# Soft-capped attention with a SoLU feed-forward block on one core: values in 32-column tiles, reciprocals of the row sums through HBM, a tabled order of steps

## The chip, the cores and the metric

The kernel runs on one core of a Trainium2 chip. Times are device microseconds (us) of one execution. The kernel before takes 423.69 us, the median of 3 runs (423.61 to 424.09). "Engines" are PE (TensorE matmul), PEld (its weight loads), DVE (VectorE), ACT (ScalarE), POOL (GpSimd) and SP (the queue that issues nearly all DMAs).

## What is computed

```
scores = (q @ k.T) / sqrt(64);  scores = cap * tanh(scores / cap)
attn   = exp(scores - max) / (sum(exp(scores - max)) + 1e-9)
x      = attn @ v                         # 4 batches, 12 heads, 448 tokens, 64 per head
h      = x @ w_in                         # 1792 x 768 times 768 x 1024
solu   = h * softmax(h)
ln     = (solu - mean) / sqrt(var + 1e-6) * g_ln
out    = ln @ w_out                       # 1792 x 1024 times 1024 x 768
```

All inputs and the output are float32.

## The kernel before, in words

The 48 heads are worked on in pairs: 24 units (6 per batch). For a unit PE makes the transposed scores of both heads in three chunks of 128 keys and one rest of 64 (`scores`, L391, `scores_rest`, L396); the scores are split into three float32r products (hi·hi, hi·lo, lo·hi), so a chunk is six matmuls in two row tiles. ACT applies tanh (L401, L419) and exp (L404). `values` (L472) multiplies the exponentials by v, one step per chunk of keys, each head in one column tile of 64; `values_rest` (L477) adds the rest. These are plain float32 matmuls, each recorded as two MATMUL records. `rowsums` (L486) multiplies the same exponentials by a selector of 32 columns, so that the row sums of head j of pair hp land in row hp of a 32-row region of one PSUM tile `z`. From unit 8 on (`ADDS_FROM`) DVE first adds the three chunks and the rest (L451, L457, L455), which leaves 4 instead of 16 row-sum matmuls for a pair of units.

`divide` ends a batch: ACT adds a guard (L535), one float32 matmul with the constant `both` (L536) adds the two regions of each head and repeats them, DVE takes reciprocals in four column parts (L541), and for each part and each of the six pairs a `stream_shuffle` (L544) spreads one row over the partitions and a multiply (L545) scales the attention output `xt`.

The feed-forward block works on 14 tiles of 128 tokens: `ff_in` splits the tile in two float32r terms (L567, L568), 36 matmuls (L577 to L579), SoLU and layer norm on DVE, ACT and POOL (L584 to L624), a transpose by DVE (L627) and four DMAs (L632, `ef<-h`); `ff_out` is 48 matmuls (L666 to L668), a copy (L675) and a store (L678). In the first batches DVE and ACT also prepare the weights (L712 to L722).

The order of all this is made when the program is built. Every piece is a step of `Plan` with an engine, a cost, a due time and the steps it needs; `Plan.run` is a list scheduler that emits the steps in the order of its own estimated starts, and each engine then works through its instructions in that order and waits where data are not ready. A step on PE also has a tile shape (`tiling`): 64x128 for scores, 128x64 for values, 128x32 for row sums, 64x64 for the rests, 128x128 for the rest of the program.

## Time and profile before

| | |
|---|---|
| median of 3 runs | 423.69 us |
| the profiled execution's own time | 423.13 us |
| its span, first to last instruction | 421.2 us |
| PE busy | 405.1 us (96%) |
| DVE busy | 298.3 us (71%) |
| ACT busy | 243.6 us (58%) |
| POOL busy | 57.6 us (14%) |

The rows further down come from the profiled execution, and sums are made against its 423.13 us. A row of a timeline gives a start, a duration and, in brackets, idle time before it and what ended that. Matmuls overlap: the distance between two starts is the price of the first, the duration is not. Busy time of PE is the union of overlapping records.

### The profile page before, as it was taken

The page shows a single profiled execution, that of the slowest core. Times are in us where ns is not written, and L with a number is a line of the kernel's source. Part 1 is how long each engine was busy: PE and PEld are TensorE (multiplying, and loading weights), DVE is VectorE, ACT ScalarE, POOL GpSimd, SP SyncE. Part 2 cuts the span into 40 slices and gives each one's busy share as a digit, 9 for nine tenths or more (in the row PEclk, how much of TensorE's full clock was granted, in tenths as well). Part 3 has the DMA queues.
Part 4 walks back from the last instruction along what each step waited for, and adds up shares of the span by engine and source line. Part 5 has one row for each costly group of instructions (what it writes and reads, how often), then busy time and mean ns, then how long its engine had stood idle before and what let it go on. Part 6 is the DMA issues. An engine that isn't in the chain of part 4 may idle for free.

```text
span 421.2 us, 6343 instructions
## 1 busy us (share of the span) xinstructions
PE 405.1 (96%) x2292; PEld 279.7 (66%) x2292; DVE 298.3 (71%) x725; ACT 243.6 (58%) x322; POOL 57.6 (14%) x122
## 2 busy tenths in 40 slices
PE   8689999999989999999999999999999999999993
PEld 4234345657734368696875696586677898998993
DVE  2999889998997899955556399964463996544510
ACT  4799998678878984625377556764911222212210
POOL 2000000144220001211130020130211101211200
PEclk9899999999999999999999999999999999999997
DMA  7878872021424230403224024031030202122031
GB/s 268 355 264 283 309 257 97 2 53 64 121 65 150 70 129 19 135 1 86 69 86 134 3 86 133 23 111 43 2 87 0 80 28 68 44 65 70 20 110 44
DMA packets 24265, 42.46 MB, mean 101 GB/s; under 512 B 3744, under 2 KB 17568, under 8 KB 24224
## 3 DMA queue, kind: packets, MB, share of 16 engines
q1 hardware_dynamic: 24080, 41.76, 31.3%
q8 instruction: 20, 0.33, 0.3%
q10 hardware_dynamic: 144, 0.20, 0.1%
q14 instruction: 21, 0.17, 0.1%
HBM read 29.10 MB, written 5.51 MB: 82 GB/s over the span
## 4 chain that ended last, share of the span: by engine, by line
PE 80%; DVE 9%; ACT 5%; POOL 2%; issue 2%; ACTq 0%; POOLq 0%; DVEq 0%
PE pv L472 11%; PE s L391 9%; PE m L666 9%; PE m L668 9%; PE m L667 9%; PE m L577 8%; PE m L579 8%; PE m L578 8%; PE s L396 4%; PE z L486 4%; DVE o L714 1%; DVE o L715 1%; PE pv L753 1%; ACT eb L404 1%; POOL st L617 1%
## 5 line engine op out<-in xcount | busy, mean ns | idle before, releaser
L666 PE MATMUL m<-wo,ln 128*128 128x384 f32 x208 | 71.2, 342 | 0.0
L668 PE MATMUL m<-wo,ln 128*128 128x384 f32 x208 | 69.9, 336 | 0.0
L667 PE MATMUL m<-wo,ln 128*128 128x384 f32 x208 | 69.7, 335 | 0.0
L577 PE MATMUL m<-wi,xh 128*128 128x512 f32 x168 | 66.4, 395 | 0.0
L579 PE MATMUL m<-wi,xl 128*128 128x512 f32 x168 | 65.8, 392 | 0.0
L578 PE MATMUL m<-wi,xh 128*128 128x512 f32 x168 | 65.7, 391 | 0.0
L600 POOL TENSOR_SCALAR st<-st 128x1 f32<-128x1 f32 x14 | 14.1, 1010 | 285.1 <-ACT ef L595 285.1
L401 ACT ACTIVATE ea<-s 128x896 f32<-128x896 f32 x48 | 41.7, 926 | 9.5 <-PE s L391 9.5
L472 PE MATMUL pv<-ea,v 128*64 128x448 f32 x192 | 42.8, 565 | 3.8 <-ACT ea L404 3.3
L675 ACT COPY o<-m 128x384 f32<-128x384 f32 x26 | 12.5, 480 | 56.3 <-PE m L668 56.3
L404 ACT ACTIVATE ea<-ea 128x1792 f32<-128x1792 f32 x24 | 41.0, 1710 | 0.3
L666 PEld LDWEIGHTS m<-wo,ln 128*128 128x128 f32 x208 | 39.0, 188 | 3.1 <-issue 1.6
L667 PEld LDWEIGHTS m<-wo,ln 128*128 128x128 f32 x208 | 39.1, 188 | 1.0 <-issue 0.4
L668 PEld LDWEIGHTS m<-wo,ln 128*128 128x128 f32 x208 | 39.0, 188 | 0.3 <-DVE ln L656 0.3
L595 ACT ACTIVATE ef<-h,st 128x1024 f32<-128x1024 f32 x14 | 16.1, 1153 | 39.6 <-DVE h L584 31.6
L577 PEld LDWEIGHTS m<-wi,xh 128*128 128x128 f32 x168 | 31.5, 188 | 9.5 <-issue 2.2
L579 PEld LDWEIGHTS m<-wi,xl 128*128 128x128 f32 x168 | 31.5, 188 | 7.0 <-DVE xl L568 0.4
L578 PEld LDWEIGHTS m<-wi,xh 128*128 128x128 f32 x168 | 31.5, 188 | 6.0
L391 PEld LDWEIGHTS s<-hi 64*128 64x128 f32 x138 | 12.9, 183 | 30.2 <-issue 13.1
L404 ACT ACTIVATE eb<-eb 128x1344 f32<-128x1344 f32 x24 | 32.2, 1341 | 0.4
L391 PE MATMUL s<-hi 64*128 64x448 f32 x138 | 30.2, 434 | 1.0 <-ACT eb L419 1.0
L472 PEld LDWEIGHTS pv<-ea,v 128*64 128x64 f32 x192 | 11.9, 138 | 26.3 <-issue 16.6
(114 smaller groups left out, 745.4 us busy)
## 6 DMA issues: line engine op xcount, KB each, us to landing
raw<-in_kq SPq DMA_DIRECT2D x24, 448.0 KB, 3.5
ef<-h SPq DMA_DIRECT2D x56, 128.0 KB, 2.7
wo<-in_w_out SPq DMA_DIRECT2D x15, 384.0 KB, 6.4
wi<-in_w_in SPq DMA_DIRECT2D x11, 512.0 KB, 7.5
v<-in_v SPq DMA_DIRECT2D x24, 224.0 KB, 2.6
out<-o SPq DMA_DIRECT2D x27, 192.0 KB, 1.9
ln<-in_w_in SPq DMA_DIRECT2D x1, 512.0 KB, 6.9
es<-in_w_out SPq DMA_DIRECT2D x1, 384.0 KB, 5.0
```

Of the source, the lines that this page charges most:

```text
L391: nc.tensor.matmul(pt.get()[:, j, :S], lhsT=x[half[j], c * P:(c + 1) * P], rhs=y[half[j], NC * P:], start=(i == 0), stop=(i == len(parts) ...
L396: nc.tensor.matmul(pt.get()[p.place[j], 0, :S], lhsT=x[half[j], :REST], rhs=x[half[j], S:], start=True, stop=True)
L401: step("ACT", act(2 * S, 0.11), at, lambda: nc.scalar.activation(out=p.chunk(c), in_=pt.get()[:, :, :S], func=AF.Tanh, scale=r_tanh), [pt] ...
L404: step("ACT", act(k * S), at, lambda: nc.scalar.activation(out=e.get(), in_=e.get(), func=AF.Exp, scale=r_exp), [e], [e])
L472: nc.tensor.matmul(t[half[j], :S], lhsT=vv[:, j * NC + c], rhs=p.chunk(c)[:, j], start=(c == 0), stop=False, skip_group_check=True)
L486: nc.tensor.matmul(zt[b].get()[r:r + 32, :S], lhsT=w, rhs=buf.get()[:, c], start=r not in zbegun[b], stop=not left[r], skip_group_check=Tr ...
L577: nc.tensor.matmul(pt.get(), lhsT=a, rhs=w[:, 0], start=(kk == 0), stop=False)
L578: nc.tensor.matmul(pt.get(), lhsT=a, rhs=w[:, 1], start=False, stop=False)
L579: nc.tensor.matmul(pt.get(), lhsT=l, rhs=w[:, 0], start=False, stop=(kk == KD - 1))
L666: nc.tensor.matmul(p, lhsT=a, rhs=w[:, 0], start=(f == 0), stop=False)
L667: nc.tensor.matmul(p, lhsT=a, rhs=w[:, 1], start=False, stop=False)
L668: nc.tensor.matmul(p, lhsT=l, rhs=w[:, 0], start=False, stop=(f == KF - 1))
```

## The change

Three things change in the work and one in its order.

- `values` makes four matmuls per chunk, each with 32 columns of v, in place of two with 64; its tile shape is then 128x32, that of the row sums.
- `divide` takes the reciprocal of all 448 columns at once into SBUF, stores them in an HBM tile `zd`, and loads them back for each part, broadcast over 64 partitions (`rs`, now one buffer for six pairs); one multiply scales a part of all six pairs. In batches whose row sums are added on DVE first (`one`: here batches 1 to 3) the `both` matmul is gone, since each head then has one region. A part is two load DMAs in batch 0 and four in batches 1 to 3.
- `ADDS_FROM` goes from 8 to 6: units 6 and 7 are added on DVE too. Only one buffer is left for `xh`.
- The order is no longer computed: `tabled` emits the steps in the order of a table, which also names the engine of each copy.

```diff
-ADDS_FROM = 8
+ADDS_FROM = 6
+XHN = 1
+RSN = 1
+ORDER = """
+01000H0W0d02WI050J03120X070Y06040Z0e0S0A0a08190fWb130g0K0B140p0c09150M0h1Z160C0DWiX70E0j1A240L180G1B0NWq1g1C0F1a1D0O0P2i
...
+    def tabled(self):
+        code = [LETTERS.index(x) for x in "".join(ORDER.split())]
+        order = [64 * x + y for x, y in zip(code[::2], code[1::2])]
+        for i in order:
+            n = self.steps[i % 2048]
+            if n["eng"] == self.COPY:
+                n["emit"](self.copy["DVE" if i >= 2048 else "ACT"])
+            else:
+                n["emit"]()
...
-    rz_r, rs_r = ring("rz", 1, [P, most]), ring("rs", 2, [P, most])
-    xh_r, xl_r = ring("xh", 2, [P, KD, P], F32R), ring("xl", XLS, [P, KD, P], F32R)
+    rs_r = ring("rs", RSN, [P, NP, most])
+    xh_r, xl_r = ring("xh", XHN, [P, KD, P], F32R), ring("xl", XLS, [P, KD, P], F32R)
...
             for j in range(2):
-                nc.tensor.matmul(t[half[j], :S], lhsT=vv[:, j * NC + c], rhs=p.chunk(c)[:, j], start=(c == 0), stop=False, skip_group_check=True)
+                for r in (0, 32):
+                    nc.tensor.matmul(t[j * D + r:j * D + r + 32, :S], lhsT=vv[:, j * NC + c, r:r + 32], rhs=p.chunk(c)[:, j], start=(c == 0), stop=False, skip_group_check=True, tile_position=(0, j * D + r))
...
-        zs, z = es_r.new(), z_r.new()
+        zs, one = es_r.new(), not general and b * NP >= ADDS_FROM
...
+        if not one:
+            z = z_r.new()
+            step("PE", MM448_F32, due, lambda: nc.tensor.matmul(z.get()[:, :S], lhsT=both, rhs=zs.get()[:, 0], start=True, stop=True), [zs], [z])
+        zd = Buf(lambda: dram.tile([P, S], F32, name=f"zd{b}"))
+        step("DVE", 0.0064 * S, due, lambda: nc.vector.reciprocal(out=zs.get()[:, 1], in_=zs.get()[:, 0] if one else z.get()[:, :S]), [zs] if one else [zs, z], [zs])
+        step("SP", 0.5, due, lambda: nc.sync.dma_start(out=zd.get(), in_=zs.get()[:, 1]), [zs], [zd], lag=2.2)
...
-                step("DVE", dve(n), due + part * LATER, lambda rs=rs, rz=rz, hp=hp, n=n: nc.vector.stream_shuffle(out=rs.get()[:, :n], in_=rz.get()[:, :n], mask=[hp] * 32), [rz], [rs])
-                step("DVE", dve(n), due + part * LATER, lambda rs=rs, hp=hp, sl=sl, n=n: nc.vector.tensor_mul(xt[b].get()[:, hp, sl], xt[b].get()[:, hp, sl], rs.get()[:, :n]), [rs, xp], [xp])
+            def spread(rs=rs, sl=sl, n=n):
+                for j in range(2):
+                    r = zd.get()[j * D:(j + 1) * D]
+                    if one:
+                        for g in range(2):
+                            nc.sync.dma_start(out=rs.get()[half[j], g::2, :n], in_=r[g * 33:g * 33 + NP - 1:2, sl].partition_broadcast(D))
+                    else:
+                        nc.sync.dma_start(out=rs.get()[half[j], :, :n], in_=r[:NP, sl].partition_broadcast(D))
+
+            step("SP", 1.7 if one else 0.9, due + part * LATER, spread, [zd], [rs], lag=2.5)
+            step("DVE", dve(NP * n), due + part * LATER, lambda rs=rs, sl=sl, n=n: nc.vector.tensor_mul(xt[b].get()[:, :, sl], xt[b].get()[:, :, sl], rs.get()[:, :, :n]), [rs, *xps], xps)
...
-        plan.run()
+        plan.run() if general else plan.tabled()
```

The table moves instructions on every engine. Three places matter below. In the rows "x2" means two such instructions in succession; line numbers of the kernel before and of the changed one differ.

The start of PE's program, before (`pv` is the output of values, `z` of row sums, `s` of scores):

```order
L753 MATMUL pv<-xtail 128x256 x5
L396 MATMUL s<-raw 64x448 x2
L386 MATMUL s<-raw 128x448 x6
L472 MATMUL pv<-ea,v 64x448 x4
L472 MATMUL pv<-eb,v 64x448 x2
L486 MATMUL z<-ea,sel 32x448 x4
L486 MATMUL z<-eb,sel 32x448 x2
L486 MATMUL z<-eb,sel_64 32x448
L486 MATMUL z<-eb,sel_65 32x448
L391 MATMUL s<-hi 128x448 x2
L391 MATMUL s<-lo,hi 128x448 x2
L391 MATMUL s<-hi,lo 128x448 x2
```

and now:

```order
L793 MATMUL pv<-xtail 128x256 x5
L429 MATMUL s<-raw 64x448 x2
L419 MATMUL s<-raw 128x448 x6
L424 MATMUL s<-hi 128x448 x2
L424 MATMUL s<-lo,hi 128x448 x2
L424 MATMUL s<-hi,lo 128x448 x2
L424 MATMUL s<-hi 128x448 x2
L424 MATMUL s<-lo,hi 128x448 x2
L424 MATMUL s<-hi,lo 128x448 x2
L506 MATMUL pv<-ea,v 32x448 x8
L520 MATMUL z<-ea,sel 32x448 x4
L520 MATMUL z<-eb,sel 32x448 x2
```

Two score chunks of unit 1 have moved ahead of the values of unit 0.

DVE between the reciprocals of batch 0 and the first multiply that uses them, now (the reciprocal, L574, stands four rows above the first of these; L759 to L768 prepare weights, L408 casts the scores' input):

```order
L408 CAST hi<-raw 128x832
L760 SCALAR_TENSOR_TENSOR o<-wo_501,o 128x384
L768 SCALAR_TENSOR_TENSOR wo_748<-o,gT,wo_748 128x384
L759 TENSOR_SCALAR o<-o 128x384
L761 SCALAR_TENSOR_TENSOR o<-wo_501,o 128x384
L760 SCALAR_TENSOR_TENSOR o<-wo_512,o 128x384
L759 TENSOR_SCALAR o<-o 128x384
L761 SCALAR_TENSOR_TENSOR o<-wo_512,o 128x384
L760 SCALAR_TENSOR_TENSOR o<-wo_620,o 128x384
L768 SCALAR_TENSOR_TENSOR wo_814<-o,gT,wo_814 128x384
L768 SCALAR_TENSOR_TENSOR wo_817<-o,gT,wo_817 128x384
L591 TENSOR_TENSOR xt<-xt,rs 128x6x128
```

Before, reciprocal, shuffles and multiplies of a part followed one another; now 14 other instructions stand between the reciprocal and the first multiply.

SP around the same place, now (`zd` is the store of the reciprocals, `rs` their loads; `v` and `raw` are loads of later units):

```order
L455 DMA v<-in_v 128x448
L401 DMA raw<-in_kq 128x896
L575 DMA zd_758<-es 128x448
L588 DMA rs<-zd_758 64x6x128 x2
L455 DMA v<-in_v 128x448
L401 DMA raw<-in_kq 128x896
L588 DMA rs<-zd_758 64x6x128 x4
L588 DMA rs<-zd_758 64x6x64 x2
L455 DMA v<-in_v 128x448
L401 DMA raw<-in_kq 128x896
```

The store and the loads of all four parts now stand between loads of `v` and `raw` for later units.

## Rows read from the trace of the kernel before

**Rows 1.** Stretches: length; PE, PEld, DVE, ACT, POOL busy; granted clock, DMA share, GB/s.

```profile
0.00:26.00 26.00, 19.69 (x94) 8.84 (x96) 18.21 (x39) 17.98 (x25) 2.71 (x22) 0.93 0.77 284
60.00:100.00 40.00, 40.00 (x223) 24.72 (x222) 38.74 (x133) 32.60 (x49) 8.20 (x11) 1.00 0.21 65
100.00:135.00 35.00, 32.53 (x191) 18.64 (x191) 30.82 (x49) 27.92 (x37) 7.95 (x12) 1.00 0.33 94
135.00:200.00 65.00, 65.00 (x383) 43.53 (x380) 52.29 (x136) 41.69 (x50) 6.57 (x14) 1.00 0.24 75
200.00:300.00 100.00, 100.00 (x573) 69.88 (x575) 67.78 (x160) 61.93 (x76) 14.77 (x24) 1.00 0.24 72
```

**Rows 2.** Timeline of PE from 5.5 us: the first unit.

```profile
13.43 2.88 PE L472 MATMUL pv<-ea,v 128*64 128x448 f32 x8 [3.01 <-ACT ea L404]
16.09 1.51 PE L472 MATMUL pv<-eb,v 128*64 128x448 f32 x4
```

**Rows 3.** The same table for 13.4 to 20 us.

```profile
13.40:20.00 6.60, 6.57 (x36) 2.24 (x38) 6.60 (x13) 4.33 (x6) 0.00 (x0) 0.74 0.98 388
```

**Rows 4.** Timeline of PE: a row-sum run of 16 records between scores and values.

```profile
34.69 0.57 PE L486 MATMUL z<-ea,sel 128*32 128x448 f32 x2
...
35.09 0.55 PE L486 MATMUL z<-ea,sel 128*32 128x448 f32 x2
...
36.35 0.97 PE L472 MATMUL pv<-eb,v 128*64 128x448 f32 x4
```

**Rows 5.** Timeline of PE: a row-sum run after DVE's adds, then two value chunks.

```profile
139.29 0.96 PE L486 MATMUL z<-es,sel 128*32 128x448 f32 x8
140.18 1.72 PE L472 MATMUL pv<-ea,v 128*64 128x448 f32 x8
141.83 0.47 PE L391 MATMUL s<-hi 64*128 64x448 f32 x2
```

**Rows 6.** Timeline of PE: the matmul with `both`, batch 1.

```profile
143.24 1.02 PE L536 MATMUL z<-es,both 128*128 128x448 f32 x2
144.19 0.97 PE L472 MATMUL pv<-eb,v 128*64 128x448 f32 x4
```

**Rows 7.** Timeline of PE: a row-sum run that waits for DVE.

```profile
125.98 1.59 PE L486 MATMUL z<-es,sel 128*32 128x448 f32 x4 [0.74 <-DVE es L455]
```

**Rows 8.** DVE's groups by line and shape: busy, mean ns | idle before.

```profile
L455 DVE TENSOR_TENSOR es<-es,eb 64x448 f32<-64x448 f32 x32 | 20.0, 625 | 0.7
L544 DVE STREAM_SHUFFLE rs<-rz 128x128 f32<-128x128 f32 x72 | 18.6, 297 | 0.0
L541 DVE RECIPROCAL rz<-z 128x128 f32<-128x128 f32 x12 | 11.4, 950 | 0.0
L568 DVE TENSOR_TENSOR xl<-xt,xh 128x768 fp32r<-128x768 f32 x12 | 11.3, 943 | 0.0
L722 DVE SCALAR_TENSOR_TENSOR wo<-o,gT,wo 128x384 fp32r<-128x384 f32 x16 | 9.5, 605 | 1.0 <-ACT wo L721 0.8
```

**Rows 9.** DMA issues: count, KB each, median us from issue to landing.

```profile
raw<-in_kq SPq DMA_DIRECT2D x24, 448.0 KB, 3.5
ef<-h SPq DMA_DIRECT2D x56, 128.0 KB, 2.7
wi<-in_w_in SPq DMA_DIRECT2D x11, 512.0 KB, 7.5
v<-in_v SPq DMA_DIRECT2D x24, 224.0 KB, 2.6
out<-o SPq DMA_DIRECT2D x27, 192.0 KB, 1.9
```

**Rows 10.** Timeline of SP: issue times.

```profile
90.02 2.62 SPq L632 DMA_DIRECT2D ef<-h  x4
```

**Rows 11.** Groups of PE's weight loads: busy, mean ns.

```profile
L472 PEld LDWEIGHTS pv<-ea,v 128*64 128x64 f32 x192 | 11.9, 138 | 26.3 <-issue 16.6 <-ACT ea L404 4.7 <-ACT eb L419 2.5
L486 PEld LDWEIGHTS z<-ea,sel 128*32 128x32 f32 x64 | 3.0, 109 | 7.4 <-issue 6.7 <-DVE h L584 0.7
```

More of the change, by code (lines that the diff above doesn't have):

```diff
@@ L114, in softcap_attention_solu @@
     nc.gpsimd.memset(mhalf, -0.5)
-    make_identity(nc, ident)
     nc.gpsimd.memset(both, 0.0)
-    for r in range(0, P, 32):
-        for c in (0, 32):
-            nc.gpsimd.tensor_copy(both[r:r + 32, r // D * D + c:r // D * D + c + 32], ident[r:r + 32, r:r + 32])
+    with tc.tile_pool(name="early", bufs=1) as early:
+        ident = early.tile([P, P], F32, name="ident")
+        make_identity(nc, ident)
+        for r in range(0, P, 32):
+            for c in (0, 32):
+                nc.gpsimd.tensor_copy(both[r:r + 32, r // D * D + c:r // D * D + c + 32], ident[r:r + 32, r:r + 32])
     nc.scalar.activation(out=acap, in_=acap, func=AF.Abs)
@@ L191, in __init__ @@
     def __init__(self, nc, free):
-        self.steps, self.free, self.tiling, self.fill = [], dict(free), None, None
+        self.steps, self.free, self.tiling = [], dict(free), None
         self.copy = {"ACT": nc.scalar.copy, "DVE": nc.vector.tensor_copy}
@@ L219, in end @@
         return max(self.free[eng], n["at"]) + n["us"][eng] + (BIAS if eng == "DVE" else 0.0)
+    def tabled(self):
+        code = [LETTERS.index(x) for x in "".join(ORDER.split())]
+        order = [64 * x + y for x, y in zip(code[::2], code[1::2])]
+        assert sorted(i % 2048 for i in order) == list(range(len(self.steps)))
+        for i in order:
[4 more added lines that the diff above has]
+                n["emit"]()
     def run(self):
@@ L269, in run @@
         assert len(order) == len(self.steps)
-        end = None
         for n in order:
-            if n["eng"] == "PE":
-                if self.fill and end is not None:
-                    self.fill(n["start"] - end)
-                end = n["start"] + n["us"]
             n["emit"]()
@@ L292, in body @@
 @with_exitstack
-def body(ctx: ExitStack, tc, kq, v, w_in, w_out, g_ln, out, r_tanh, r_exp, mhalf, sel, sels, ident, gT, xtail, both, guard, general, const=None, loaded=None):
+def body(ctx: ExitStack, tc, kq, v, w_in, w_out, g_ln, out, r_tanh, r_exp, mhalf, sel, sels, gT, xtail, both, guard, guard2, general, const=None, loaded=None):
     nc = tc.nc
@@ L335, in body @@
     m_r = ring("m", 2, [P, 512], F32, ps)
-    plan = Plan(nc, dict(SP=1.2, ACT=3.5, DVE=3.9, PE=1.2, POOL=4.0))
+    plan = Plan(nc, dict(SP=1.2, ACT=3.5, DVE=3.9, PE=1.3, POOL=4.0))
     step = plan.step
@@ L533, in divide @@
         due = begin[b + 1] + EARLY
-        zs, z = es_r.new(), z_r.new()
-        step("ACT", act(S, 0.05, 1), due, lambda: nc.scalar.activation(out=zs.get()[:, 0], in_=zt[b].get()[:, :S], func=AF.Identity, bias=guard), [zt[b]], [zs])
-        step("PE", 0.76, due, lambda: nc.tensor.matmul(z.get()[:, :S], lhsT=both, rhs=zs.get()[:, 0], start=True, stop=True), [zs], [z])
+        zs, one = es_r.new(), not general and b * NP >= ADDS_FROM
+        step("ACT", act(S, 0.05, 1), due, lambda: nc.scalar.activation(out=zs.get()[:, 0], in_=zt[b].get()[:, :S], func=AF.Identity, bias=guard2 if one else guard), [zt[b]], [zs])
@@ L538, in divide @@
         for part, sl in enumerate(cuts[b]):
             n = sl.stop - sl.start
-            rz = rz_r.new()
-            step("DVE", 0.0064 * n, due + part * LATER, lambda rz=rz, sl=sl, n=n: nc.vector.reciprocal(out=rz.get()[:, :n], in_=z.get()[:, sl]), [z], [rz])
-            for hp in range(NP):
-                rs, xp = rs_r.new(), xpart[b][part][hp]
-                step("DVE", dve(n), due + part * LATER, lambda rs=rs, rz=rz, hp=hp, n=n: nc.vector.stream_shuffle(out=rs.get()[:, :n], in_=rz.get()[:, :n], mask=[hp] * 32), [rz], [rs])
-                step("DVE", dve(n), due + part * LATER, lambda rs=rs, hp=hp, sl=sl, n=n: nc.vector.tensor_mul(xt[b].get()[:, hp, sl], xt[b].get()[:, hp, sl], rs.get()[:, :n]), [rs, xp], [xp])
+            rs, xps = rs_r.new(), xpart[b][part]
```

53 lines of the change are left out of this document (32 added, 21 removed).

## The prediction

> **What bounds the kernel now.** I read the table by stretch first, then the timeline of PE, then DVE's groups and the DMA issues. From 60 to 100 us and from 135 to 300 us PE is busy all the time, 40.0 of 40, 65.0 of 65, 100.0 of 100 us [rows 1]: there the end is set by what stands in PE's program, and work that another engine loses is worth nothing by itself. PE is idle in two places that can be won back: 6.3 us of the first 26 (26.0 less 19.69; 1.3 of it lie before the first instruction) and 2.5 us between 100 and 135 (35.0 less 32.53) [rows 1]. In the first, PE waits 3.01 us for ACT's exp before the first values [rows 2], and behind that wait the granted clock is 0.74 of full over 13.4 to 20 us [rows 3], which means that part of it ran at the lower of the two levels, 1.2 GHz instead of 2.4: eight value records take 2.88 us, the next four 1.51 [rows 2], where the same eight take 1.72 and four 0.97 later [rows 5, 6]. That is 1.7 us more. In the second, DVE and ACT are the late ones; a row-sum run waits for DVE's add in the middle [rows 7], and DVE is busy 30.8 of these 35 us, 38.7 of the 40 before [rows 1]. So DVE matters up to about 135 us and hardly after it.
>
> **The change on PE.** Distances between starts are the prices.
>
> *Row sums of units 6 and 7.* A run of 16 records lasts from 34.69 to 36.35, 1.66 us [rows 4]; a run of eight after DVE's adds from 139.29 to 140.18, 0.89 us [rows 5]. Two of the first kind become one of the second: 2 x 1.66 - 0.89 = 2.4 us off.
>
> *The matmul with `both`.* Three of four go. Between scores and values it costs 143.24 to 144.19, 0.95 us [rows 6]; inside feed-forward work no change of tile shape goes with it, and I count 0.75, two records at the 0.375 us spacing of float32 records (34.69 to 35.09 holds one with its entry, 0.40) [rows 4]. 0.95 + 2 x 0.75 = 2.45 us off.
>
> *Changes of tile shape.* Two value chunks last 1.65 us (140.18 to 141.83) [rows 5]; four records at 0.375 are 1.50, so the change of shape behind them costs 0.15. Counted in the two orders, PE's shape changes 139 times before and 120 times now. Two of the 19 are in the terms above; 17 x 0.15 = 2.55 us off.
>
> *Values in four tiles.* 72 chunks now have eight records in four column tiles. The trace has no such matmul for values, but the row sums have the same shape, 128x32 with 448 columns: their four tiles start within 0.03 us and the next four 0.40 us after them [rows 4]. Lower bound: nothing, the four run side by side as now the two. Upper bound: two pairs one after the other, 0.75 us more per chunk, 54 us. I take nothing, since the row-sum run is the same shape in the same engine.
>
> Sum on PE's program: 2.4 + 2.45 + 2.55 = 7.4 us off.
>
> **Stalls.** The two score chunks that now stand ahead of the first values fill 1.2 us of the 3.0 us wait (two chunks and the change of shape behind them take 141.83 to 143.24, 1.41 us [rows 5, 6], so a chunk is some 0.6). What is left is split in short waits, and I expect the clock to stay up: 1.7 us more. I take 3.0 us off at the start; bounds 0 (ACT is as late, and the clock falls as before) and 6.7 (all idle time and the 1.7). Between 100 and 135 us I take 2.5 us off, all the idle time, since DVE sheds work: shuffles of 128 columns alone were 18.6 us over four batches [rows 8]. Against it stand the adds for units 6 and 7, two halves of 0.625 and two whole adds of twice the columns, an estimate of 3.5 us per unit, 7 us [rows 8]. Bounds: 0 and 3.5 with the refills of PE behind each wait.
>
> **The trip through HBM.** It is a new wait. Reciprocals of 448 columns take 3.5 times 0.95, 3.3 us at most, in one piece [rows 8]; a store of 224 KB lands after about 1.9 us, as the stores of 192 KB do, or 2.6 like a load of 224 KB [rows 9]; then two loads of 192 KB (four of 96 KB from batch 1) are issued at 0.65 each (four in 2.62) [rows 10], and the last lands 2.6 to 3.5 us after its issue, like `v` or like `raw` [rows 9]; the multiply of 768 columns takes 0.94 like the subtraction of that size [rows 8]. Reciprocal to first scaled part: 3.3 + 1.9 + 0.65 + 2.7 + 0.94, about 9.5 us, where before a reciprocal of 0.95, six shuffles at 0.3 and six multiplies of the same columns were done after some 4.5. What covers it: on DVE 14 instructions stand between the reciprocal and the first multiply, at most 8.5 us if all took the 0.605 of the weight steps [rows 8], rather 6 to 7 since several are shorter; the trip needs 5.3. So DVE, which works in order, hardly waits. On PE, from the matmul with `both` to the first feed-forward matmul stand four score chunks (2.4 us), five value chunks (3.75), a rest (0.75) and their shape changes, about 7.7 us by the prices above; the chain that feeds it is 9.5 and 2 us for the split in two terms, 11.5. So PE is 3.5 to 4 us short once, in batch 0, where before it was not idle [rows 1]. I add 3.0 (some of it hides in DVE work that was late anyway); bounds 0 and 6. In batches 1 to 3 feed-forward tiles of the batch before cover the trip. If that cover were gone, it would cost the same 4 us three more times.
>
> On SP the loads of later parts wait until the multiply before them frees the one `rs` buffer, and loads of `v` and `raw` for later units are queued behind them. A part takes about 5 us (1.3 issue, 2.7 landing, 0.94 multiply), so `raw` behind three parts comes up to 15 us later than it could, and feed-forward tiles of 36 matmuls stand between the units that need it. I price that at nothing; if that cover fails, PE waits for a split once or twice, within the bound of 6 above.
>
> **Sum.** -7.4 - 3.0 - 2.5 + 3.0 = -9.9 us. From the profiled 423.13 us that is 413.2. The median of the runs lies 0.56 above the profiled execution, so I forecast 413.8.
>
> **Rivals.**
>
> *The stalls stay.* The table only moves them: PE's program is 7.4 us shorter, the first batch's trip costs 3.0 to 6, nothing is won at the start. 423.7 - 7.4 + 3 = 419.3. For it: DVE is 97% busy from 60 to 100 us [rows 1] and the adds for units 6 and 7 fall into that stretch. Against it: the start's order plainly puts ready work ahead of the wait.
>
> *All idle time goes.* The trip is covered and the waits are too: -7.4 - 6.7 - 2.5, 407.
>
> *Four tiles cost more than two.* Eight weight loads per chunk take 8 x 0.109 = 0.87 us, more than the chunk's 0.75; now four take 4 x 0.138 = 0.55 [rows 11]. If they ran one after another, 72 x 0.12 = 8.6 us come back: 422, the same within the measurement or just faster. Against it: the 16 loads of the row-sum run, 1.74 us, fit into 1.66 us with its matmuls [rows 4, 11]. The Trainium skill ("TensorEngine Tiling (Array Packing)", Instruction Overhead) goes the same way: about 60 cycles for each matmul, so that 144 more matmuls would be, as an estimate from that page, 3.6 us at 2.4 GHz. By that rule the sum would be 6.3 us off and the time 417; the row-sum run speaks against it, since its four tiles keep the spacing of two.
>
> *The trip is late every time (the other side).* DVE works in order, so when a part lands late, everything queued behind its multiply waits: splits, score inputs, copies out of PSUM; PE follows. The cover between multiplies is some 4 to 5 us of DVE work. It decides from a landing of about 4 us on. If loads broadcast in runs of 512 bytes landed like the weights of the loaded start, 7.5 us [rows 9], 16 parts would each be 3 us or more late, 48 us on DVE, of which PE feels a half where DVE is full and less later: 15 to 25 us, so 428 to 438. Against it: the queue is a quarter busy after 60 us [rows 1], and `ef`, short runs of 1 KB, lands after 2.7 [rows 9]. [...]
>
> *The change does not do what it says* could only mean that the two pairs of value tiles run one after the other, +54 us less 10: 467.
>
> **How the numbers follow.** About 0.2% is what a measurement can tell from no change, 0.85 us. Forecast (410 to 416.5): 0.52. The stalls stay (416.5 to 420.5): 0.20. All idle time goes (below 410): 0.13. Four tiles cost more: 0.05, half of it within 0.2%. Late trip: 0.08, mostly slower. Serial tiles: 0.02. Faster 0.88, same 0.03, slower 0.09. The range is 408 to 420.5: it leaves out a part of the best case, the tile rivals and the late trip.
>
> **What would show it.** In the profile after: value records at 0.375 us spacing with eight per chunk; `both` once; no wait of 3 us before the first values, and a granted clock near 1.00 from 13 to 20 us; PE idle near 60 to 85 us and nowhere else for more than 1 us; `rs` landing in 2.5 to 3.5 us; DVE's busy time below 280 us. I am wrong if value chunks start more than 0.8 us apart in a run, if DVE waits for `rs` in most parts, or if PE's idle time between 26 and 135 us is above 8 us.

## The result and the profile after

The changed kernel takes **426.53 us**, the median of 20 runs; the kernel before, on the same chip, 423.75 (422.85 to 424.56). Nineteen of the 20 took 424.31 to 428.60 us; one took 2194.01, for which nothing here gives a reason, and it is left out of the ratio. The ratio is **1.0072, interval 1.0058 to 1.0086**: slower by 0.7%, outside the range of 408 to 420.5. The profiled execution took 427.35 us (span 425.5, mean granted clock 0.979), 4.2 us more than that of before.

The same table by stretch as in [rows 1], of the kernel after:

```profile
0.00:26.00 26.00, 20.33 (x118) 9.62 (x120) 16.60 (x36) 16.71 (x21) 2.69 (x22) 0.87 0.75 262
26.00:60.00 34.00, 32.17 (x294) 13.00 (x290) 33.92 (x67) 33.95 (x46) 0.00 (x0) 1.00 0.89 298
60.00:100.00 40.00, 31.80 (x158) 19.03 (x154) 35.12 (x65) 24.83 (x38) 1.68 (x3) 0.87 0.31 100
100.00:135.00 35.00, 34.73 (x257) 19.73 (x257) 29.53 (x48) 31.65 (x40) 8.87 (x15) 1.00 0.34 91
```

From 60 to 100 us, where PE had been busy for 40.0 us of 40, it is busy for 31.8, and the granted clock falls from 1.00 to 0.87. From 100 to 135 the idle time is gone, as forecast. DVE and ACT stand at 33.9 of 34 us between 26 and 60. The line of that stretch in the kernel before, which stood in no group ahead:

```profile
26.00:60.00 34.00, 33.48 (x248) 12.84 (x246) 31.31 (x60) 33.94 (x45) 0.00 (x0) 1.00 0.90 310
```

The whole can be booked by the distances between starts on PE, as in the prediction: each record is priced at the distance that it has where nothing waits. The prices of PE's program add up to 394.5 us before and 387.1 after: **7.4 us less, the forecast sum**. (Where exactly the undisturbed price is set moves both sums by up to 2 us, and their difference hardly at all.) What lies between starts and isn't in these prices I call **lost time** (waits, the refill behind a wait, records at half clock; the expectations below call it PE's idle time). With the 1.3 us ahead of PE's first matmul, prices and lost time make up the start of its last. It rises from 18.3 to 30.6 us, by 12.3; 12.3 less 7.4 is the 4.9 us by which PE's last matmul comes later (418.97 against 414.09; what follows it is 0.7 us shorter). By stretch, with each wait booked where the record ahead of it starts:

| lost time, us | 0–26 | 26–60 | 60–100 | 100–135 | later | all |
|---|---|---|---|---|---|---|
| before | 9.6 | 1.1 | 0.4 | 4.9 | 2.1 | 18.3 |
| after | 8.7 | 3.2 | 13.5 | 0.9 | 4.3 | 30.6 |

**The start.** The timeline of SP's queue, first of before, then of after (start, length, line, operation):

```profile
1.18 0.42 SPq L368 DMA_DIRECT2D raw<-in_kq  x1
```

```profile
0.72 0.39 SPq L131 DMA_DIRECT2D acap<-in_cap  x1
4.62 0.82 SPq L401 DMA_DIRECT2D raw<-in_kq  x2
```

The first load of `raw` is issued 3.44 us later. What SP waited for, by the waits of SP after, and what POOL does then, by its timeline:

```profile
SPq L164 <- DVE guard L153: 3.1, 1, 3.1
```

```profile
2.06 1.54 POOL L144 COPY both<-ident 32x32 f32<-32x32 f32 x8
```

This comes from a part of the change that the cut diff ahead of the prediction leaves out. The identity matrix, from which `both` is made, moved from the constant pool into a pool `early` that is closed after the copies:

```diff
-    ident = const.tile([P, P], F32, name="ident")
-    make_identity(nc, ident)
+    with tc.tile_pool(name="early", bufs=1) as early:
+        ident = early.tile([P, P], F32, name="ident")
+        make_identity(nc, ident)
+        for r in range(0, P, 32):
+            ...
```

Two things then stand ahead of the first `raw` load. In the trace it waits for a semaphore of POOL, as the loads of before and of e1 (below) do not; from this and from the diff I infer that the first `raw` buffer got the closed pool's memory. POOL's copies end at 3.6 us. And on SP the reading of the capped flag (L164), which waits for DVE, has moved ahead of it: it ends at 4.57 us, where before it came at 25 us. So the reading is what ends last; why it moved with the pool no run shows. PE then starts and goes on like this (timeline of PE after, answering to [rows 2, 5]):

```profile
8.49 1.76 PE L429 MATMUL s<-raw 64*64 64x448 f32 x4 [3.17 <-DMA raw<-in_kq]
...
17.59 1.71 PE L506 MATMUL pv<-ea,v 128*32 128x448 f32 x16 [0.71 <-ACT ea L437]
...
66.64 0.74 PE L424 MATMUL s<-lo,hi 64*128 64x448 f32 x2 [3.35 <-DVE lo L409]
...
68.81 3.21 PE L506 MATMUL pv<-ea,v 128*32 128x448 f32 x16
...
76.40 1.71 PE L506 MATMUL pv<-ea,v 128*32 128x448 f32 x16 [1.46 <-ACT ea L437]
```

Three things are to be seen. The two score chunks ahead of the first values did what they were to do: the wait there is 0.71 us instead of 3.01, and the values run at full clock at once, 1.71 us. The values in four tiles cost what they cost in two: two chunks, now 16 records, take 1.71 us, against 1.72 for the eight of before [rows 5]. And at 66.64 there is a wait that before did not have, for the `lo` of unit 7's scores, behind which the same 16 value records take 3.21 us: from 66.6 to 72.2 us the granted clock is 0.50, the lower of the two levels. DVE at that time (its timeline after):

```profile
62.73 2.98 DVE L574 RECIPROCAL es<-z 128x448 f32<-128x448 f32 x1
65.59 0.99 DVE L409 TENSOR_TENSOR lo<-raw,hi 128x832 fp32r<-128x832 f32 x1
...
72.24 0.98 DVE L591 TENSOR_TENSOR xt<-xt,rs 128x768 f32<-128x768 f32 x1
```

The reciprocal of batch 0, now in one piece, stands ahead of `lo` in DVE's queue. The last line is the first multiplication, 9.5 us behind the start of the reciprocal. The longest waits of PE from 26 to 100 us:

```profile
PE m L623 <- DVE xh L613: 3.4, 1, 3.4
PE s L424 <- DVE lo L409: 3.4, 1, 3.4
PE pv L506 <- ACT ea L437: 1.5, 1, 1.5
```

In the same view of before there is only one wait:

```profile
PE pv L472 <- ACT xt L502: 0.5, 1, 0.5
```

**The trip.** The DMA issues after, answering to [rows 9]:

```profile
raw<-in_kq SPq DMA_DIRECT2D x24, 448.0 KB, 3.8
...
v<-in_v SPq DMA_DIRECT2D x24, 224.0 KB, 3.6
out<-o SPq DMA_DIRECT2D x27, 192.0 KB, 1.9
rs<-zd SPq DMA_DIRECT2D x38, 96.0 KB, 3.0
rs<-zd SPq DMA_DIRECT2D x6, 192.0 KB, 3.7
```

and the view of the tile `rs`, which has the spread of the landings, and how long its readers waited:

```profile
  DVE xt L591: 13.4, 9
...
DMA to landing us min/median/max: 2.6/3.1/6.3
```

DVE waited nine times for a part, 13.4 us in all. Only one of these waits, of 0.6 us, falls in batch 0; the other eight, 12.8 us, come after 100 us, where no wait in the view of PE's waits is longer than 0.6 us, so they hardly reach PE. In batch 0 SP issues part 1, then waits with `v` and `raw`, and part 2 follows 7.4 us later (timeline of SP):

```profile
67.75 1.37 SPq L588 DMA_DIRECT2D rs<-zd  x2
74.21 0.33 SPq L455 DMA_DIRECT2D v<-in_v  x1
74.59 0.42 SPq L401 DMA_DIRECT2D raw<-in_kq  x1
75.19 15.17 SPq L588 DMA_DIRECT2D rs<-zd  x6
```

### The profile page after: what moved, and what is told of

Read it like the earlier page. It is cut to its first block, busy times and chain, and to the rows that moved or that the text cites. A ratio compares the mean times of both kernels' runs of the same rounds, so it can differ in the third digit from the quotient of the medians.

```text
span 425.5 us, 6702 instructions
## 1 busy us (share of the span) xinstructions
PE 402.0 (94%) x2550; PEld 279.3 (66%) x2550; DVE 291.9 (69%) x469; ACT 229.8 (54%) x303; POOL 54.7 (13%) x122
## 4 chain that ended last, share of the span: by engine, by line
PE 75%; DMA 8%; ACT 7%; DVE 4%; issue 2%; SPq 2%; POOL 1%; ACTq 0%; DVEq 0%; POOLq 0%
PE pv L506 10%; PE m L712 9%; PE m L714 9%; PE m L713 9%; PE s L424 8%; PE m L623 8%; PE m L625 8%; PE m L624 8%; DMA raw<-in_kq 4%; PE s L429 4%; PE z L520 2%; ACT ea L434 2%; ACT ea L437 2%; DMA es<-in_w_out 1%; ACT o L758 1%
## 5 line engine op out<-in xcount | busy, mean ns | idle before, releaser
L434 ACT ACTIVATE ea<-s 128x896 f32<-128x896 f32 x48 | 41.8, 917 | 15.0 <-PE s L424 14.7
L506 PE MATMUL pv<-ea,v 128*32 128x448 f32 x384 | 43.0, 561 | 4.0 <-ACT ea L437 2.2
L721 ACT COPY o<-m 128x384 f32<-128x384 f32 x24 | 11.3, 481 | 59.6 <-PE m L714 59.5
L646 POOL TENSOR_SCALAR st<-st 128x1 f32<-128x1 f32 x14 | 11.0, 784 | 243.5 <-ACT ef L641 243.5
L623 PEld LDWEIGHTS m<-wi,xh 128*128 128x128 f32 x168 | 31.9, 190 | 12.3 <-DVE xh L613 3.8
L625 PEld LDWEIGHTS m<-wi,xl 128*128 128x128 f32 x168 | 31.8, 189 | 7.4 <-DVE xl L614 0.6
L624 PEld LDWEIGHTS m<-wi,xh 128*128 128x128 f32 x168 | 32.0, 190 | 6.1
L424 PEld LDWEIGHTS s<-hi 64*128 64x128 f32 x138 | 13.1, 187 | 30.2 <-issue 8.6
L424 PE MATMUL s<-lo,hi 64*128 64x448 f32 x138 | 26.1, 374 | 3.4 <-DVE lo L409 3.4
```

The source lines that it names most:

```text
L424: nc.tensor.matmul(pt.get()[:, j, :S], lhsT=x[half[j], c * P:(c + 1) * P], rhs=y[half[j], NC * P:], start=(i == 0), stop=(i == len(parts) ...
L434: step("ACT", act(2 * S, 0.11), at, lambda: nc.scalar.activation(out=p.chunk(c), in_=pt.get()[:, :, :S], func=AF.Tanh, scale=r_tanh), [pt] ...
L506: nc.tensor.matmul(t[j * D + r:j * D + r + 32, :S], lhsT=vv[:, j * NC + c, r:r + 32], rhs=p.chunk(c)[:, j], start=(c == 0), stop=False, sk ...
L623: nc.tensor.matmul(pt.get(), lhsT=a, rhs=w[:, 0], start=(kk == 0), stop=False)
L624: nc.tensor.matmul(pt.get(), lhsT=a, rhs=w[:, 1], start=False, stop=False)
L625: nc.tensor.matmul(pt.get(), lhsT=l, rhs=w[:, 0], start=False, stop=(kk == KD - 1))
```

## The experiments

Ratios are to the kernel before, measured beside each; lost times are of one profiled execution each, and move by one or two us with the clock.

### The start

**e1_ident_kept**: the changed kernel with the identity back in the constant pool.

```diff
-    with tc.tile_pool(name="early", bufs=1) as early:
-        ident = early.tile([P, P], F32, name="ident")
...
+    ident = const.tile([P, P], F32, name="ident")
...
```

> The changed kernel with one thing undone: the identity stays in the constant pool instead of a short-lived one, so no later buffer lies over it. Theory S (the first load of scores input waits at the start for the copies that read the identity, 4.62 us instead of 1.18): the first load is issued near 1.2 us, PE's rests of unit 0 start near 5.9 us instead of 8.5, everything up to 60 us comes 2.5 to 3.5 us earlier, and the time falls by as much, to about 423.3. Rival H (the start is hidden: DVE, ACT and the weight loads fill 26 to 60 us anyway): PE's start moves but the time stays within 1 us of 426.5.

Measured: 422.64 us, ratio 0.9974 [0.9954, 0.9994]. Against 1.0072 that is 4.1 us won by this edit alone. The first load is issued early again (SP's timeline of e1):

```profile
1.17 0.89 SPq L400 DMA_DIRECT2D raw<-in_kq  x2
```

Lost time before 26 us is 5.3, against 9.6 before and 8.7 after.

**e8_before_early**: the other way round, the kernel before with the identity in a closed pool and nothing else.

```diff
-    ident = const.tile([P, P], F32, name="ident")
...
+    with tc.tile_pool(name="early", bufs=1) as early:
+        ident = early.tile([P, P], F32, name="ident")
...
```

> The kernel before with one edit: the identity matrix lies in a pool that is closed after its copies, as in the change. On SP the reading of the capped flag, which waits for DVE, and a wait for POOL then stand ahead of the first kq load, as in the changed kernel. Theory S (the closed pool alone makes the start late, by the 3.44 us between issues at 1.18 and 4.62 us): 426.0 to 429.0, idle time of PE up only before 26 us or just behind it, no row of half speed that before lacks. Rival C (the late start also costs through what it shifts, the lower clock above all): over 429. Rival N (the pool does nothing in a kernel with the planner): 423 to 424.5.

Measured: 428.26 us, ratio 1.0101 [1.0084, 1.0118], 4.3 us slower. SP's timeline:

```profile
4.59 0.34 SPq L368 DMA_DIRECT2D raw<-in_kq  x1
```

Lost time rises from 18.3 to 23.3, nearly all in front (9.6 to 12.7 before 26 us, 1.1 to 2.9 up to 60). Put in or taken out, the closed pool costs 4.1 to 4.3 us. This part of the cause is shown; how much of it is the wait for POOL and how much the reading of the flag, both of which come with the pool, is not told apart.

### What makes PE wait from 26 to 100 us

With the start mended, 13.1 us are lost there in e1, against 1.5 before. (The two stretches have 7.9 and 5.2, but the first of these has the wait for `lo` from 60.2 to 63.3 us, since the record ahead of it starts at 59.8.) The longest waits of PE in e1 from 26 to 100 us:

```profile
PE s L423 <- DVE lo L408: 3.2, 1, 3.2
PE m L622 <- DVE xh L612: 1.8, 1, 1.8
PE pv L505 <- ACT ea L436: 1.4, 1, 1.4
PE pv L505 <- ACT xt L535: 1.3, 2, 1.0
```

With the smaller ones of that view, 5.4 us of waits end with DVE, 3.4 with ACT and 0.2 with a DMA; the other 4 us are refills and half clock. First the edits that were run with the late start still in:

**e3_shuffle_batch0**: batch 0 takes its reciprocals by 24 shuffles on DVE, not through HBM.

```diff
+        local = b == 0 and not general
...
+                if local:
+                    for hp in range(NP):
+                        nc.vector.stream_shuffle(out=rs.get()[:, hp, :n], in_=zs.get()[:, 1, sl], mask=[hp] * 32)
```

> The changed kernel, same table, but in batch 0 alone no trip through HBM: the store and the loads are left out and each multiply is preceded by six shuffles of the SBUF reciprocals. Theory T (the trip in batch 0 makes PE's stalls between 60 and 100 us, 13.5 us): DVE has 24 shuffles more, about 5 us, yet PE's stall before the second feed-forward tile (3.4 us) goes and the time falls by 4 to 8 us, to 418.5 to 422.5. Rival D (DVE is what is late there, with weights and reciprocals): the 5 us more on DVE show on PE and the time stays or grows, 426 to 430.

Measured: 430.60 us, ratio 1.0171 [1.0147, 1.0195], 4 us above the change. Without the trip PE loses 15.5 us from 60 to 100, more than with it.

**e7_rs_first**: in SP's order `v` and `raw` go behind part 2 of `rs`.

```diff
+        for what, where in [([449, 459], 330)]:
+            taken = [next(i for i in order if i % 2048 == w) for w in what]
+            order = [i for i in order if i not in taken]
+            k = next(k for k, i in enumerate(order) if i % 2048 == where) + 1
+            order[k:k] = taken
```

> The changed kernel with two entries of the table moved: on SP the loads of part 2 of batch 0 stand ahead of the loads of v and raw that waited for PE until 74.2 us, instead of behind them. Theory Q (queue order on SP makes the trip long: part 2 is issued at 75.2 behind raw and lands after 6.2 us): part 2 is issued near 73.3 and lands in about 3.7 us, the second multiply comes 4 to 5 us earlier, PE's wait of 3.4 us before the second tile goes, and the time falls by 3 to 5 us, to about 422.5. Theory T without Q (the landing itself is slow): the multiply comes at most 2 us earlier and the time falls by under 1.5 us. Rival D: no change.

Measured: 428.17 us, ratio 1.0117 [1.0092, 1.0142]; 13.8 us lost from 60 to 100. The edit did its work on SP: part 2 now lands 3.4 to 3.9 us after its issue instead of 6.3. Nothing is won by it, so the queueing on SP is not the cause.

**e6_lo_first**: the same lines with `([326], 418)`, which puts the reciprocal of batch 0 behind unit 7's `lo` on DVE.

> The changed kernel with one entry of the table moved: on DVE the subtraction that makes the low scores input of unit 7 stands ahead of the one-piece reciprocal of batch 0 instead of behind it. If the wait of 3.35 us that PE has for that subtraction (66.6 us) is a loss of its own, it goes and the time falls by 2.5 to 4 us with the half-clock stretch behind it, to 422.5 to 424. Theory T says that the trip then starts 1 us later and the loss is found again before the first feed-forward tiles: within 1.5 us of 426.5.

Measured: 426.25 us, ratio 1.0054 [1.0031, 1.0077], the change's own time within the intervals; of the 13.5 us, 11.1 are left.

**e4_ident_shuffle** is e1 and e3 together, **e9_ident_lo** e1 and e6.

> The changed kernel with the identity in the constant pool and batch 0 spread by 24 shuffles on DVE in place of the trip through HBM; the other batches go through HBM as in the change. Theory T (batch 0's trip makes a good part of the idle time from 60 to 100 us in e1_ident_kept, 5.2 us, the wait for rs and xh): 419 to 421.5. Rival D (DVE is full there, the shuffles' 5 us on it cost what the trip did): 422 to 426, idle time from 60 to 100 us 5 to 9.

> The changed kernel with two edits: the identity in the constant pool (as e1_ident_kept, 422.64) and the 2.95 us reciprocal of batch 0 behind the lo of the next unit (as e6_lo_first). Theory D (the reciprocal in one piece holds up the scores of the next unit, 3.2 us of waiting at 62 us in e1_ident_kept): the wait of PE for lo falls below 1 us and the time by 1.5 to 3, to 419.5 to 421.2, PE's idle time between 26 and 100 us from 13.1 to 10 or 11. Rival H (DVE has more to do than fits there, so the wait only moves to xh and the batch-0 feed-forward): 422 to 423.5, that idle time 12 to 14.

Measured: e4 425.68 us, ratio 1.0041 [1.0023, 1.0059]; e9 421.53 us, ratio 0.9941 [0.9919, 0.9963]. So with either start the shuffles in batch 0 are some 3 to 4 us worse than the trip, which fits a DVE that has no room for them. The reciprocal behind `lo` is worth about 1.4 us (0.9974 to 0.9941, intervals that overlap a little); of the lost 13.1 us it leaves 14.7 in the profiled execution, so its gain is not to be read there. Its expected 10 or 11 was a miss. PE's waits for `lo` do fall, to 1.1 us in two, but those for `ea` from ACT rise from 1.4 to 3.5: most of the wait has only moved.

**e17_recip_split** cuts batch 0's reciprocal in two, 128 columns where it was and 320 behind the issue of the first `rs` load, each with a store of its own; **e18_recip_split_early** also moves the first multiplication six steps up on DVE.

```diff
+        cut = CUTS0[0] if b == 0 and not general else S
...
+            def rest():
+                nc.vector.reciprocal(out=zs.get()[:, 1, cut:], in_=z.get()[:, cut:S])
+                nc.sync.dma_start(out=zd2.get()[:, cut:], in_=zs.get()[:, 1, cut:])
```

> e1_ident_kept with batch 0's reciprocal in two pieces, columns 0 to 127 where it was, the other 320 behind the issue of the first rs load, each with its own store to HBM; the result is the same. Theory R (the piece of 2.95 us ahead of lo made the 3.2 us of PE's waiting at 60 us, and delays the first part's trip by 2 us): that wait falls to 1.5 or less, PE's idle time between 26 and 100 us to 8 to 10.5, time 419.5 to 421.5. Rival Z (DVE has the same work before the feed-forward, so PE waits later instead): 422 to 424.

> e17_recip_split with the first multiplication of batch 0 six steps earlier in DVE's order, in front of the pieces of w_out that stood ahead of it. Theory R: 0 to 2 us below e17_recip_split, the first ff_in matmul at 70 to 71 us instead of 73.3. Rival Z: within 0.5 us of e17, or above it where DVE waits for the load.

Measured: e17 420.91 us, ratio 0.9942 [0.9924, 0.9961]; e18 423.14 us, ratio 0.9982 [0.9967, 0.9997]. DVE's timeline of e17:

```profile
59.13 0.98 DVE L577 RECIPROCAL es<-z 128x128 f32<-128x128 f32 x1
59.99 0.99 DVE L410 TENSOR_TENSOR lo<-raw,hi 128x832 fp32r<-128x832 f32 x1
...
63.73 2.15 DVE L581 RECIPROCAL es<-z 128x320 f32<-128x320 f32 x1
```

The longest wait for `lo` falls from 3.2 us to 1.2, the lost time from 13.1 to 12.3, the longest of it now waits for `ea` from ACT (3.6 us in two). Multiplying earlier is worse: the next `lo` on DVE comes at 71.8 us instead of 70.1, and PE's longest wait for `ea` grows from 2.6 to 3.8. e17 and e9 are the fastest kernels here that compute everything, 0.6% below the kernel before.

**e10_ident_planner**: e1's work with the order made by `Plan.run` in place of the table.

```diff
-        plan.run() if general else plan.tabled()
+        plan.run()
```

> The changed kernel with the identity in the constant pool and with its order made by the planner, as before, in place of the table: the work of the change without the order of the change. Theory O (the table's order makes the idle time between 26 and 100 us, 13.1 us in e1_ident_kept, by what it puts ahead on DVE): that idle time falls below 8, time below 420. Rival W (the work makes it: row sums added on DVE, the trip through HBM): 11 to 16 of idle time, 421.5 to 425. Rival P (the planner, whose costs don't know the trip's delays, is worse than the table): over 425.

Measured: 462.61 us, ratio 1.0902 [1.0875, 1.0929]; 67.4 us are lost, with waits for `xh` ahead of feed-forward tiles of 14.9 us in two, the longest 11.8. With this work the table is worth 40 us against this planner. That no third order does better is not shown.

**e16_sums_on_pe**: e1 with the row sums of units 6 and 7 on PE again, without DVE's adds.

```diff
+        here = paired and u < 8
...
-            step("DVE", dve(2 * S), due + SUMA * d, lambda: nc.vector.tensor_add(t.get(), p.chunk(0), p.chunk(1)), [p.ea], [t])
+            step("DVE", dve(2 * S), due + SUMA * d, lambda: None if here else nc.vector.tensor_add(t.get(), p.chunk(0), p.chunk(1)), [p.ea], [t])
...
+            if here and c == NC - 1:
+                g = hp % 2
+                for j in range(2):
+                    for i, (buf, cc, one) in enumerate(((p.ea, j, sel), (p.ea, 2 + j, sel), (p.eb, j, sel), (p.eb, 2, sels[p.place[j].start // D]))):
+                        row = j * D + g * 32
+                        nc.tensor.matmul(zt[b].get()[row:row + 32, :S], lhsT=one[:, NP - 1 - hp:NP - 1 - hp + 32], rhs=buf.get()[:, cc], start=row not in zbegun[b], stop=False, skip_group_check=True, tile_position=(0, row))
```

> e1_ident_kept with the row sums of units 6 and 7 on PE again, 8 matmuls a unit behind the unit's last value tile, and without their additions on DVE; the rest as in the change, and the result is the same. PE's program gets longer by some 1.1 us. Theory U (the additions, 5.8 us of DVE between 86 and 97 us, hold the exponentials' buffer, so that PE has nothing to put between the batch-0 feed-forward's waits): time 420 to 422.3. Rival V (they stand where DVE has room by then): 423 to 425.

Measured: 427.94 us, ratio 1.0103 [1.0085, 1.0121]. The edit costs PE far more than the 1.1 us expected: to fit the later layout, each half's four matmuls stand behind each other in one column tile. PE's timeline of e16:

```profile
69.51 1.67 PE L514 MATMUL z<-ea,sel 128*32 128x448 f32 x4
71.01 0.54 PE L514 MATMUL z<-eb,sel 128*32 128x448 f32 x1
...
72.55 1.67 PE L514 MATMUL z<-eb,sel 128*32 128x448 f32 x4
74.14 0.59 PE L428 MATMUL s<-raw 64*64 64x448 f32 x2
```

16 records take 4.6 us here, 1.66 in four column tiles [rows 4]. So it doesn't tell what the adds cost on DVE; that stays open.

**Taking work away.** Five kernels on e1 take work from one queue or from several; what they compute is no longer the right result. e12 leaves out the instruction that gives w_out its signs (DVE), e13 the `rs` loads of batch 0, e15 both; e20 leaves out the exponentials of units 3 to 7 (ACT), e19 all three.

The signs of e12 (`sign` is the instruction that stood there), the loads of e13 (in `spread`; the multiplication takes `xt` in place of `rs`) and the exponentials of e20:

```diff
+        step("DVE", dve(n), due, sign if src is w_in else lambda: None, [st, y], [y])
```

```diff
             def spread(rs=rs, sl=sl, n=n):
+                if b == 0 and not general:
+                    return
```

```diff
-            step("ACT", act(k * S), at, lambda: nc.scalar.activation(out=e.get(), in_=e.get(), func=AF.Exp, scale=r_exp), [e], [e])
+            step("ACT", act(k * S), at, lambda: None if 3 <= u < 8 and not general else nc.scalar.activation(out=e.get(), in_=e.get(), func=AF.Exp, scale=r_exp), [e], [e])
```

> e1_ident_kept without the instruction that puts the sign back into each piece of w_out (DVE, 0.55 us each, some 15 of them between 45 and 95 us): those weights lose their signs. It takes 8 us of work from DVE and leaves everything else. Theory D (DVE has more to do ahead of 93 us than fits, and PE's idle time between 26 and 100 us, 13.1 us, is waiting for DVE's results): that idle time falls to 6 to 9 and the time to 416 to 419. Rival T (the trip through HBM and its one buffer set the pace there): 421 to 423.5, the idle time 11 to 14.

> e1_ident_kept with no rs loads in batch 0: its four multiplications of 0.95 us stay and take xt itself in place of rs, so batch 0 isn't divided by its row sums and nothing waits for the trip; the reciprocal and its store stay. Theory T (the trip in batch 0 sets PE's idle time between 60 and 100 us, 5.2 us, and holds up what follows): 417 to 420. Theory D (DVE is the late one): within 1.5 us of e1_ident_kept, 421 to 423.5.

> e12_less_dve and e13_no_trip together: no sign instruction for w_out on DVE, and no rs loads in batch 0. Theory B (DVE's queue and the trip stand side by side, each alone hidden by the other): PE's idle time between 60 and 100 us falls below 4 (5.2 in e1, 8.2 in e12, 11.4 in e13) and the time is 416.5 to 419. Rival A (a third thing holds PE there, ACT or the order of PE's own queue): 420 to 422.5, that idle time over 5.

> e1_ident_kept without the exponentials of units 3 to 7 (ACT, 1.7 and 1.3 us a unit, 15 us in all between 33 and 95 us); the tanh stays and its results are summed. Theory A (ACT's queue, full from 26 to 60 us, is what makes PE wait there): PE's idle time between 26 and 100 us from 13.1 to 6 to 9, time 416 to 419.5. Rival D (DVE alone, ACT only waits with it): 421 to 423.5.

> e15_less_no_trip and e20_no_exp together: less on DVE by the signs of w_out, no rs loads in batch 0, no exponentials in units 3 to 7. Theory L (three limits side by side, each hiding the others; what is left of them is the shortened PE program that finds nothing ready): PE's idle time between 26 and 100 us below 6 (12.5 in e15), time 411 to 415. Rival O (the order of the queues itself, which no lighter work mends): 417 to 420.

| kernel | taken away | us | ratio | below e1 | lost, 26–100 |
|---|---|---|---|---|---|
| e1 | – | 422.64 | 0.9974 [0.9954, 0.9994] | – | 13.1 |
| e13 | trip | 422.72 | 0.9970 [0.9954, 0.9986] | 0.2 | 14.4 |
| e20 | exponentials | 421.43 | 0.9943 [0.9924, 0.9962] | 1.3 | 13.9 |
| e12 | signs | 420.98 | 0.9933 [0.9918, 0.9949] | 1.7 | 16.2 |
| e15 | trip, signs | 419.55 | 0.9907 [0.9883, 0.9931] | 2.8 | 12.5 |
| e19 | all three | 417.43 | 0.9859 [0.9845, 0.9874] | 4.9 | 8.2 |

("Below e1" is the difference of the ratios times 423.6 us, known to about 1 us.) Each one alone is worth little, against every expectation that named it as the limit. The three sum to 3.2 us apart and give 4.9 together; the intervals are too wide to call that more than the sum. The lost time speaks for it, in one execution each: no kernel with one thing taken away loses less than e1, and the one without all three loses 4.9 us less.

What hides what can be seen in two waits. In e13, without any trip, DVE reaches the first multiplication 9.5 us after the start of the reciprocal, as in the changed kernel and in e1 (9.6), and PE's wait for `xh` is 1.9 us against 1.8: the work that stands in between on DVE takes as long as the trip (in e1 the first part lands at 69.0 us, and DVE comes to it at 69.05). When DVE sheds 8 us (e12), it waits 1.6 us for a part, PE's longest wait becomes the one for `xh`, 3.6 us, and when the trip goes too (e15), it falls to 0.4. So **three limits stand side by side** in the stretch, DVE's queue, ACT's queue and the trip; that each is partly hidden by the others is what these waits suggest, and not shown by the times. With all three lightened PE is busy for 35.4 of the 40 us from 60 to 100, against 33.2 in e1, and the clock stays at 1.00 (table by stretch and waits of PE from 26 to 100 us, both of e19):

```profile
60.00:100.00 40.00, 35.44 (x206) 22.81 (x204) 37.74 (x66) 25.26 (x41) 5.57 (x10) 1.00 0.19 60
```

```profile
PE s L423 <- DVE lo L408: 3.5, 2, 2.8
```

The wait that is left is the one behind the reciprocal in one piece. The time expected of e19, 411 to 415, was missed by 2.4 us, and 8.2 us are still lost where under 6 were expected. 417.43 lies in the range of its rival, the order of the queues itself, which these experiments leave open.

**e11_pool_wi, e14_pool_both**: a try at giving DVE room with nothing left out, the subtractions for the low halves of w_in (e11), and of 14 pieces of w_out (e14) on POOL.

```diff
-            step("DVE", dve(n), due, lambda: nc.vector.tensor_sub(lo(), yf(), hi().bitcast(F32)), [y, part], [w])
+            step("DVE", dve(n), due, lambda: (nc.vector if general else nc.gpsimd).tensor_sub(lo(), yf(), hi().bitcast(F32)), [y, part], [w])
```

> e1_ident_kept with the low halves of the w_in pieces (DVE L763, 0.69 us each for 128x512) subtracted on POOL, which does nothing between 26 and 60 us; the result is the same. Theory D: 7 to 8 us less for DVE ahead of 50 us, PE's idle time between 26 and 100 us from 13.1 to 7 to 10, time 417 to 420.5. Rival P (POOL takes over 1.5 us a piece and holds up the staging buffers, or slows DVE): 422 to 427. Rival T: 421.5 to 423.5.

> e11_pool_wi and besides the low halves of the first 14 w_out pieces (DVE L767, 0.61 us each) as two instructions on POOL. Theory D: another 8 us off DVE between 48 and 92 us, time 1 to 3 less than e11_pool_wi, 415 to 419. Rival P (POOL's two instructions, over 1 us each, hold up the staging buffers): over e11_pool_wi by 1 to 6.

Measured: e11 426.49 us, ratio 1.0071 [1.0056, 1.0087]; e14 441.00 us, ratio 1.0404 [1.0391, 1.0418]. Groups by line and shape, of POOL in e11 from 20 to 60 us, and of DVE from 26 to 50 us in e11 and then in e1:

```profile
L763 POOL TENSOR_TENSOR wi<-o,wi 128x512 fp32r<-128x512 f32 x9 | 16.5, 1846 | 16.3 <-DVE wi L762 8.7 <-ACT ea L433 3.5 <-ACT eb L451 2.6
```

```profile
L759 DVE SCALAR_TENSOR_TENSOR o<-wi,o 128x512 int32<-128x512 int32 x5 | 4.5, 899 | 0.0
L758 DVE TENSOR_SCALAR o<-o 128x512 int32<-128x512 int32 x6 | 4.4, 732 | 0.2 <-ACT o L757 0.2
```

```profile
L759 DVE SCALAR_TENSOR_TENSOR o<-wi,o 128x512 int32<-128x512 int32 x5 | 3.5, 693 | 0.0
L758 DVE TENSOR_SCALAR o<-o 128x512 int32<-128x512 int32 x5 | 2.1, 425 | 0.2 <-ACT o L757 0.2
```

A piece takes 1.85 us on POOL, and beside it these two instructions of DVE get longer by 30 and 70%. Others do not: the cast that makes the high half (L762) stays at 0.42 us. Of the room that was made for DVE nothing is left: it is busy for 33.6 of the 34 us from 26 to 60, as in e1 (33.8). Where the further 14.5 us of e14 go is open.

## Why the prediction was wrong

**Right.** PE's program: -7.4 us, all of it there, with its three terms (139 shape changes to 120, one `both`, the row sums). The values in four tiles at no cost. The stall of 100 to 135 us: 4.9 us lost before, 0.9 after, against my 2.5. The score chunks ahead of the first values: with the start mended lost time there falls by 4.3 us against my 3.0, and the clock keeps up. The sizes of the trip: reciprocal 2.98 us (at most 3.3), store 1.95 (1.9), issue 0.61 each (0.65), landing 3.0 for 96 KB and 3.7 for 192 KB (2.6 to 3.5), multiplication 0.96 (0.94), and 9.5 from the reciprocal to the first multiplication (9.5), with DVE not idle before it. Batches 1 to 3 covered on PE; SP's queueing worth nothing (e7).

**Wrong, first step: "I take 3.0 us off at the start; bounds 0 ... and 6.7".** The bounds left out a loss. The order of SP after shows the reading of the flag ahead of the first load, and the diff shows a pool that is closed before the body's pool opens; I costed neither. It is 4.1 to 4.3 us by e1 and e8. This step alone turns the sign, for without it the change is 0.26% faster; but 422.64 us would still be outside the range.

**Wrong, second step: "there the end is set by what stands in PE's program".** It was said of 60 to 100 us and of 135 to 300; the stretch from 26 to 60 I left out altogether. From 135 us on it nearly holds (2.1 us lost before, 4.3 after). From 26 to 100 us PE was busy nearly all the time, but so were the others: ACT for 33.94 of the 34 us from 26 to 60, DVE for 31.3 of these 34 (the line is shown with the result) and 38.7 of the next 40 [rows 1]. PE's share could be cut there without the end coming nearer. In e1 PE reaches unit 7's scores at 59.8 us instead of 64.3, and the first feed-forward matmul at 73.3 instead of 68.3. What was saved is waited for: of gains of 4.3 us (start), 7.4 (program) and 3.8 (100 to 135 us), 11.6 are lost again from 26 to 100 us and 2.6 later, which leaves about 1.5 (PE's last matmul comes 1.6 us earlier than before; 1.1 by the ratio). I had seen that DVE matters there, and used it only for a rival ("The stalls stay", 419.3), which still counted the whole 7.4. That DVE "sheds work" fails in this stretch: it is busy for 70.1 us from 26 to 100 before and for 72.0 in e1, and over the whole program for 291.9 in the changed kernel, where I had named under 280. My own sign of being wrong came out too: PE is idle for 10.3 us between 26 and 135 us by the table of stretches, and I had named 8.

**Mis-sized: "The trip through HBM ... I add 3.0 ... bounds 0 and 6".** The wait for `xh` is 3.4 us in the changed kernel and 1.8 in e1, close to my 3.0. But I looked for the price in the trip alone. The chain's other end, the reciprocal in one piece, sits in DVE's queue ahead of `lo` and PE waits 3.2 to 3.35 us for that `lo`, with half clock behind it; I had counted the reciprocal's length in the chain and not what is queued behind it. Taken out of the way (e6, e9, e17) it wins at most some 1.4 us, so it is not the whole of the loss. Nor is the trip: in its place the shuffles lose more (e3, e4), and without it alone nothing is won (e13).

**The range** left no more than 9 in 100 for slower, nearly all of it on a late trip in every batch. Neither cause of the loss was among the rivals.

**Open:** how the loss from 26 to 100 us divides among the three queues, for the kernel without all three still loses 8.2 of e1's 13.1 us there; how much of it DVE's adds for units 6 and 7 make (e16 failed to tell); and whether another order of this work would do without the waits, since only single moves in the table were tried.

## What to carry to other kernels

Read what each queue has ahead of its first load before you price a start: here closing a scratch pool early put the wait for its last reader, and the reading of a flag, ahead of the first load, for 1% of the time. Where two or three engines are full at once, a shorter program on one of them is worth only what the others leave; price it stage by stage, and take work from all of them in an experiment before you call one the limit. Look at what is queued behind an instruction of 3 us, and not only at its own chain: here PE waited 3.2 us behind one, though cutting it in two won only some 1.4 us of the time, since the next wait was close.

## What the runs showed of the hardware that was not expected

- A subtraction of 128x512 that takes DVE 0.69 us takes POOL 1.75 us on average over its twelve, and two of DVE's integer instructions beside it go from 0.69 to 0.90 and from 0.43 to 0.73 us, while a cast of the same size stays at 0.42 (e11).
- Four column tiles of 128x32 run fully side by side, for values as for row sums (16 records in 1.71 us); 16 row-sum records ordered one column tile after the other take 4.6 (e16).
- A store of 224 KB into HBM landed in 1.9 to 2.3 us, and a broadcast load from it in 3.0 for 96 KB and 3.7 for 192 KB (medians). Two of 192 KB that were issued just behind a load of `raw` took 6.2 and 6.3; with that load moved behind them (e7) they took 3.4 and 3.9.
- Behind a wait of 3.35 us the granted clock was 0.50 for over 5 us, and 16 value records took 3.21 us instead of 1.71: there the lower clock adds 1.5 us, nearly half of the wait itself.
